# A two-lane recurrent transformer on one core: from a hand-staged schedule with DRAM round trips to an order list-placed at build time

## The chip, the cores and the metric

The kernel runs on one core of one Trainium2 chip. The metric is the device time of one execution in microseconds (us); lower is better. A core has TensorE (PE; its weight loads are shown as PEld), VectorE (DVE), ScalarE (ACT), GpSimd (POOL) and SyncE (SP, which here only issues DMAs). Each engine runs its own instructions in order and waits for the others by semaphores.

## The reference, cut to what matters

Four layers, A B A B, each added to its input. All weights are bf16; both A layers use the same weights, and so do both B layers.

```python
def _A_ref(x, mem0, Wq, Wk, Wv, Wo, seg_len):      # 2048 rows in 64 segments of 32, 32 heads of 192, model width 640
    mem = mem0                                      # 8 memory rows
    for s in range(n_seg):
        h = concatenate([mem, xs])                  # 8 + 32 = 40 rows
        q, k, v = h @ Wq, h @ Wk, h @ Wv            # 640 -> 6144 each
        p = softmax(where(mask, q @ k.T * scale, -1e9))
        o = (p @ v) @ Wo                            # 6144 -> 640
        mem = o[:M]                                 # the next segment needs it
        outs.append(o[M:])

def _B_ref(x, w1, w2, w3, w4):                      # 640 -> 640 -> 640, 640 -> 1536 -> 640
    h = gelu(layernorm(x) @ w1)
    hs = (four column groups of h, shifted by +1, -1, +2, -2 rows) @ w2
    x1 = x + hs
    return x1 + gelu(layernorm(x1) @ w3) @ w4

x = x + A(layernorm(x)); x = x + B(layernorm(x)); x = x + A(layernorm(x)); x = x + B(layernorm(x))
```

The memory makes layer A a recurrence over 64 segments: no segment can start before the one ahead of it has its first eight output rows.

## The kernel before

**Two lanes.** A step t runs segment t of the first A layer (lane 0) together with segment t - 6 of the second A layer (lane 1, `D_LAG` = 6). Both use the same weights, so the 2 x 40 rows form one moving operand of 80 columns. There are 64 + 6 = 70 steps. In the first six and the last six steps only one lane has a segment; the width stays 80.

**A step** goes over 8 groups of 4 heads. For a group, `st_proj` makes q and k transposed (30 matmuls of 80 columns each, L530) and v (10 matmuls of 384 columns, L568); `st_scores` adds the mask by a matmul of the identity with a constant (L600) and the scores (L610); `st_softmax` takes the row maximum (DVE, L617), its negative (L619), four exponentials with their sums (ACT, L624), reciprocal and product (DVE, L630 and L632); `st_pt` transposes P (L642) and copies it to SBUF (ACT); `st_pv` makes the heads' output (L654, L659), which DVE copies to `oT`; `st_wo` adds 30 matmuls of 80 columns to `psy` (L675), a PSUM tile that lives for the whole step and is cleared by a matmul with zeros (L515). The stages of neighbouring groups are interleaved by hand. `a_finish` copies the memory columns of `psy` into the next step's `hT` (ACT, L494); the next step's first q and k wait for that.

**Layer B** runs every second step on a chunk of 64 rows of each lane (128 rows), cut into stages that stand as fillers behind the groups (`b2x_stages`). The rows go through DRAM: `a_xnew` transposes the step's output back, adds the residual and stores it to `x1d` or `x3d` (SP queue); a later chunk loads it again as `xw` (ACT queue, `sA`), takes two layer norms in a row, and stores its result to `x2d`, which lane 1 loads again as `xs1`.

**Weights.** Wq, Wk, Wv and Wo are cut into 64 half-group units of 480 KB; 37 stay in SBUF after their first load (`get_w`, L357), 27 are streamed in every step. Ahead of the first step the 27 are copied inside DRAM to `wS`, where a partition's 3840 bytes lie together (`nc.scalar.dma_start`, ACT queue); the streams read `wS` (L362). The weights of B are copied to `wB` likewise and streamed per chunk in 13 pieces (L334). All streams use one ring of six 480 KB buffers, `wst`, and the SP queue.

**Order.** The instructions stand in each engine's queue in about the order in which Python issued them; `tc.high_priority()` lifts `a_finish`. What the fillers load and compute is thereby fixed against the groups. An SP instruction whose buffer isn't free holds what stands behind it, and a DVE instruction whose DMA hasn't landed holds every later DVE instruction.

Of the kernel before, what the change touches and what calls it, by code (L numbers as in the profile page):

```python
# [14 lines left out]
B2X = 1  # L15
D_LAG = 6 if B2X else 4
HG = 4
# [5 lines left out]
RING_BUFS = 6  # L23
N_RES_HALVES = 37 if B2X else 26
B_SLOT_SHIFT = 0
B_LOAD_Q = "act"
RELAYOUT = 1
LAZY_RES = 1
PT_EARLY = 0
LN_SPLIT = 1  # L30
B_SHARED_RING = 1
RINGB_BUFS = 2
RES_GROUP0_FIRST = 0
SM_ACCUM = 1
PIPE_DEEP = 1
V_TRANSPOSE = 0
PREP_DMA_Q = "sp"
LN_NORM_POOL = 0
DEFER_XNEW = 1
OT_EVAC_ENG = "dve"  # L40
KT_EVAC_ENG = "dve"
B_WSTAT = 0
HS_SEQ = 1
XROW_DELAY = 0
KZ_ENG = "dve"
XS_MERGE = 0
DBG_T_LIMIT = 0
DBG_DO_A = 1
DBG_DO_B = 1
DBG_PRINT_POOLS = 0  # L50
# [3 lines left out]
def kernel(  # L54
# [26 lines left out]
    assert Dm % P == 0 and F % P == 0 and Dh == 192 and H % HG == 0 and HG == 4  # L81
    assert SEG == 32 and M == 8 and S % SEG == 0
    assert Dm % 4 == 0 and (Dm // 4) % 32 == 0
# [3 lines left out]
    XS = 2 * SEG  # L87
    NS = XS + 2 * M
    MS = [XS, XS + M]
    XP = XS + 8  # L90
    scale = float(Dh) ** -0.5
    T_A = NSEG + D_LAG
    T = NSEG + D_LAG + (3 if B2X else 2)
    if B2X:
        assert D_LAG % 2 == 0 and NSEG % 2 == 0
    NP2 = NSEG // 2
    XB = 2 * XS
    WB2 = XS + 4
    WSZ = KC * GW
    assert WSZ == GC * Dm  # L100
    QD = Dm // 4
    WB = SEG + 4
    WBP = WB + 4

    def head_pieces(i):
        f0, f1 = Dh * i, Dh * (i + 1)
        res = []
        f = f0
        while f < f1:
            c = f // P  # L110
            p0 = f % P
            p1 = min(P, p0 + (f1 - f))
            res.append((c, p0, p1))
            f += p1 - p0
        return res

    PIECES = [(i, c, p0, p1) for i in range(HG) for (c, p0, p1) in head_pieces(i)]
    STRAD = sorted(set(c for (i, c, p0, p1) in PIECES if p1 - p0 < P))
    assert STRAD == [1, 4]
    SIDX = {c: n for n, c in enumerate(STRAD)}  # L120

    def w2_pieces():
        offs = [1, 3, 0, 4]
        res = []
        for gi in range(4):
            f, f1 = QD * gi, QD * (gi + 1)
            while f < f1:
                kc = f // P
                p0 = f % P
# [98 lines left out]
    def _cons_order():  # L228
# [11 lines left out]
        for g in range(NG):  # L240
            if g + 1 < NG:
                A(g + 1)
# [949 lines left out]
```

## Time and profile before

| | |
|---|---|
| median of 3 runs | 4447.67 us (4444.01 to 4458.48) |
| profiled execution, span of its instructions | 4440.8 us |
| PE busy | 3858.8 us (87%), 72349 matmuls |
| DVE / ACT / POOL busy | 2650.4 / 1988.4 / 578.7 us |
| DMA | 1232.59 MB, mean 278 GB/s |
| mean granted TensorE clock | 0.951 |

The profiled execution's own time isn't listed beside its span; the three runs lie 3.2 to 17.7 us above the span, the median 6.9 us. Times in a row of the timeline are microseconds from the first instruction: start, duration, engine, line, operation, what it writes and reads, shapes, count, and in brackets how long the engine had been idle and what ended that. A row may merge several instructions. A matmul's end is modelled; what counts for a stream of them is the distance from one start to the next.

### The profile page before, as it was taken

The page shows a single profiled execution, that of the slowest core. Times are in us where ns is not written, and L with a number is a line of the kernel's source. Part 1 is how long each engine was busy: PE and PEld are TensorE (multiplying, and loading weights), DVE is VectorE, ACT ScalarE, POOL GpSimd, SP SyncE. Part 2 cuts the span into 40 slices and gives each one's busy share as a digit, 9 for nine tenths or more (in the row PEclk, how much of TensorE's full clock was granted, in tenths as well). Part 3 has the DMA queues.
Part 4 walks back from the last instruction along what each step waited for, and adds up shares of the span by engine and source line. Part 5 has one row for each costly group of instructions (what it writes and reads, how often), then busy time and mean ns, then how long its engine had stood idle before and what let it go on. Part 6 is the DMA issues. An engine that isn't in the chain of part 4 may idle for free. (4 is left out here: it accounts for less than half of the span.)

```text
span 4440.8 us, 168838 instructions
## 1 busy us (share of the span) xinstructions
PE 3858.8 (87%) x72349; PEld 3433.7 (77%) x72420; DVE 2650.4 (60%) x7089; ACT 1988.4 (45%) x7427; POOL 578.7 (13%) x1578
## 2 busy tenths in 40 slices
PE   2898989899889898888888889888889988999995
PEld 2787878788778787777787778787788877888883
DVE  1455656666666666665666666666566666566554
ACT  1444444444444444444444444444444444444442
POOL 2111111111111111111111111111111111111110
PEclk7999999999999999999999999999999999999997
DMA  9887878888788888887878888788788888888784
GB/s 357 296 275 250 275 270 278 283 287 283 270 284 284 287 283 276 276 286 268 282 271 282 284 286 280 273 273 273 268 280 278 282 284 292 282 280 276 267 279 161
DMA packets 404193, 1232.59 MB, mean 278 GB/s; under 512 B 47080, under 2 KB 88176, under 8 KB 403440
## 3 DMA queue, kind: packets, MB, share of 16 engines
q1 hardware_dynamic: 378632, 1190.97, 78.6%
q10 hardware_dynamic: 21016, 23.76, 1.7%
q8 instruction: 566, 9.27, 0.8%
q0 software_dynamic: 3792, 7.05, 0.5%
q14 instruction: 187, 1.53, 0.1%
HBM read 1202.10 MB, written 38.50 MB: 279 GB/s over the span
## 5 line engine op out<-in xcount | busy, mean ns | idle before, releaser
L624 ACT ACTIVATE Pm<-pss,nb 80x80 bf16<-80x80 f32 x2240 | 699.6, 320 | 297.7 <-DVE nb L619 210.6
L568 PEld LDWEIGHTS <-hT 128*80 128x80 bf16 x5600 | 616.6, 118 | 209.5 <-issue 2.4
L372 ACT CAST V<-psv 80x384 bf16<-80x384 f32 x1120 | 507.2, 479 | 358.3 <-PE psv L568 278.4
L568 PE MATMUL psv<-wv,hT 128*80 128x384 bf16 x3500 | 663.5, 327 | 0.8 <-DMA wv<-in_A_Wv_dram 0.7
L374 DVE CAST oT<-pso 128x480 bf16<-128x480 f32 x560 | 367.7, 657 | 476.1 <-PE pso L659 474.0
L530 PEld LDWEIGHTS <-wst 128*128 128x128 bf16 x14700 | 637.3, 104 | 4.1 <-DMA wst<-wS 3.1
L374 DVE CAST kT<-psk 128x480 bf16<-128x480 f32 x560 | 364.8, 651 | 421.0 <-PE psk L530 419.3
L592 POOL COPY Vz<-V 80x128 bf16<-80x128 bf16 x560 | 169.7, 303 | 2878.0 <-ACT V L372 2865.6
L530 PE MATMUL psq<-hT,wq 128*128 128x80 bf16 x10500 | 496.9, 207 | 30.1 <-ACT hT L494 17.9
L530 PEld LDWEIGHTS <-wq 128*128 128x128 bf16 x10500 | 455.0, 103 | 38.7 <-issue 29.3
L372 ACT CAST qT<-psq 128x480 bf16<-128x480 f32 x560 | 307.5, 549 | 386.3 <-PE psq L530 384.6
L675 PE MATMUL psy<-oT,wst 128*128 128x80 bf16 x7350 | 360.2, 204 | 122.6 <-DVE oT L374 121.0
L675 PE MATMUL psy<-oT,wo 128*128 128x80 bf16 x9450 | 444.8, 204 | 2.1 <-DMA wo<-in_A_Wo_dram 2.1
L624 ACT ACTIVATION_READ_ACCUMULATOR Pm<-pss,nb 80x1 f32 x2240 | 442.5, 198 | 0.0
L675 PEld LDWEIGHTS <-wst 128*128 128x128 bf16 x7350 | 317.6, 101 | 151.2 <-issue 146.9
L568 PE MATMUL psv<-wst,hT 128*80 128x384 bf16 x2100 | 417.0, 330 | 0.8 <-DMA wst<-wS 0.8
L530 PE MATMUL psk<-hT,wst 128*128 128x80 bf16 x8400 | 411.9, 206 | 1.8 <-DMA wst<-wS 1.8
L530 PE MATMUL psk<-hT,wk 128*128 128x80 bf16 x8400 | 408.1, 205 | 3.0 <-DMA wk<-in_A_Wk_dram 3.0
L675 PEld LDWEIGHTS <-wo 128*128 128x128 bf16 x9450 | 387.5, 102 | 2.7 <-DMA wo<-in_A_Wo_dram 2.6
L372 ACT COPY PT<-pst 80x320 bf16<-80x320 bf16 x560 | 242.4, 433 | 273.2 <-PE pst L642 224.7
L610 PEld LDWEIGHTS <-qT 128*80 128x80 bf16 x3360 | 228.1, 123 | 170.5 <-issue 116.6
L374 DVE CAST kTz<-psk 64x160 bf16<-64x160 f32 x1120 | 351.9, 314 | 10.3
(122 smaller groups left out, 5892.4 us busy)
## 6 DMA issues: line engine op xcount, KB each, us to landing
wst<-wS SPq DMA_DIRECT2D x1890, 480.0 KB, 4.9
wst<-wB SPq DMA_DIRECT2D x395, 480.0 KB, 5.2
wst<-wB SPq DMA_DIRECT2D x71, 320.0 KB, 4.5
x1d<-xs SPq DMA_DIRECT2D x64, 80.0 KB, 4.0
xs<-x2d SPq DMA_DIRECT2D x64, 80.0 KB, 3.6
x3d<-xs SPq DMA_DIRECT2D x64, 80.0 KB, 3.7
xw<-x1d ACTq DMA_DIRECT2D x31, 160.0 KB, 3.6
x2d<-xw SPq DMA_DIRECT2D x31, 160.0 KB, 5.5
```

The lines of the kernel that those rows point to most:

```text
L372: nc.scalar.copy(out=out_ap, in_=in_ap)
L374: nc.vector.tensor_copy(out=out_ap, in_=in_ap)
L530: nc.tensor.matmul(out=psq[:, c, :], lhsT=w[:, kc, cc * P:(cc + 1) * P], rhs=hT[:, kc, :], start=(kc == 0), stop=(kc == KC - 1))
L568: nc.tensor.matmul(out=psv[:], lhsT=hT[:, kc, :], rhs=wv[:, kc, :], start=(kc == 0), stop=(kc == KC - 1))
L592: nc.gpsimd.tensor_copy(out=vz[:, :, 0, 0:64], in_=V3[:, SS, 0:64])
L610: nc.tensor.matmul(out=o_, lhsT=l_, rhs=r_, start=False, stop=(n == len(ops) - 1))
L624: nc.scalar.activation(out=E[:, i, :], in_=pss[:, i, :], func=ACT.Exp, bias=nb[:], scale=scale, accum_out=sums[:, i:i + 1])
L675: nc.tensor.matmul(out=cx.psy[:, m, :], lhsT=wo[:, cc, m * P:(m + 1) * P], rhs=oT[:, c, :], start=False, stop=last)
```

## The change

The kernel is rewritten around a build-time planner; what is computed stays the same.

- **Recording and placement.** `Plan.add` records each operation with its engine, an assumed duration, a due time and the buffers that it reads and writes. `Plan.place` then fixes the order on all engines: it goes forward in assumed time, and of the operations of an engine that could start soonest it takes the one with the earliest due time. A load is assumed to take 1.6 us, its size at 350 GB/s and 0.4 us. Only the order is kept; on the chip the engines still wait by semaphores.
- **Lanes.** The lag is 5, so there are 69 steps. Memory and segment of a lane lie together (40 columns), and a step with one lane uses 40 columns only (steps 0 to 4 and 64 to 68).
- **Mixer rows on chip.** The step's output columns go from `psy` to `yTB` (DVE). A chunk transposes `yTB` and adds the residual `xres`, which POOL loaded. The two layer norms in a row become one pass with two scale columns. `x1d` and `x3d` are gone. Lane 1's new columns are written to `hT` straight from the chunk's result (`chunk_end`); `x2d` remains, in bf16, as the residual. Lane 0's next two segments are normalised and transposed with the chunk.
- **Weights.** No copy in DRAM: both resident and streamed units are read from the input tensors, whose contiguous runs are 768 bytes (q, k, v, w1, w3) or 1280 bytes (Wo, w2, w4). Only w1 is copied once, to `w1d` (POOL), with its columns in another order. The ring is split: five buffers for A (`RING_A`), one for B (`RING_B`). B has 12 units per chunk, w2 now in five column groups rather than eight pieces; the second w2 unit takes five DMAs.
- **Smaller things.** The mask is added by DVE in one operation with scaling and minimum (`tensor_tensor_reduce`), in place of the mask matmul, the maximum and its negative. The zero matmul for `psy` is gone: the first Wo matmul starts the tile. K and V are written once in a layout that holds zeros where the heads of 192 straddle 128 partitions; POOL's two copies per group (`Vz`) are gone. PSUM is split by class (`PSUM_POOLS`).

```diff
-D_LAG = 6 if B2X else 4
...
-RING_BUFS = 6
-N_RES_HALVES = 37 if B2X else 26
...
-RELAYOUT = 1
...
-    x1d = dram.tile([S, Dm], f32, name="x1d")
...
-            nc.scalar.dma_start(out=w_view(wS[stream_idx[u_]], kind), in_=w_src(kind, g, hf))
...
-        nc.tensor.matmul(out=cx.psy[:], lhsT=zer[:, :], rhs=zer[:, 0:1].to_broadcast([P, KC * NS]),
-                         start=True, stop=False)
...
-        nc.tensor.matmul(out=pss[:], lhsT=ident[0:NS, 0:NS], rhs=maskb[:], start=True, stop=False)
...
-                stores.append(lambda: nc.sync.dma_start(out=x1d[SEG * segs[0]:SEG * (segs[0] + 1), :], in_=xo[0:SEG, :]))
...
-                {"sp": nc.sync, "act": nc.scalar, "pool": nc.gpsimd}[B_LOAD_Q].dma_start(
-                    out=xw[2 * j0 + Lb:2 * j1:2, :], in_=src[t0_ + j0:t0_ + j1, :])
-                if kp < NP2:
-                    nc.gpsimd.dma_start(out=xl_c[Lb:4:2, :], in_=src[TOK * kp + TOK - 2:TOK * kp + TOK, :])
...
+LAG = 5
+HG = 4
+N_RES = 37
+RING_A = 5
+RING_B = 1
+STEP = 48.0
+PSUM_POOLS = {"y": 1, "P": 3, "S": 2, "B": 2}
+OT_BUFS = 4
+V_BUFS = 3
+LAT = 0.2
+PE_LAT = 0.25
+DMA_RATE = 350.0e3
...
+                lim = m + (0.12 if e == "PE" else 0.05)
+                s, o = min((so for so in vals if so[0] <= lim), key=lambda so: (so[1].due, so[1].i))
...
+            if o.dma:
+                srv = max(s + 1.6, srv) + o.dma / DMA_RATE
+                done = srv + 0.4
...
+                if o.dma:
+                    at = done
+                elif x.e == e:
+                    at = o.end
+                else:
+                    at = o.end + (PE_LAT if e == "PE" else LAT)
...
+            return resident[u]
+        b = Slotted("ra", None)
+        b.make = lambda: wring.tile([P, HSZ], bf16, name="wst", tag=f"ra{b.slot}")
+
+        def fn(op):
+            nc.sync.dma_start(out=w_view(T(b), kind), in_=w_src(kind, g, hf))
+        add("SP", 0.06, due, fn, w=(b,), dma=P * HSZ * 2, queue="wa")
...
+    def load_b(nm, a, e, due):
...
+        b = Slotted("rb", None)
+        b.make = lambda: wring.tile([P, HSZ], bf16, name="wstB", tag=f"rb{b.slot}")
...
+        ln = lanes(t)
+        both = len(ln) == 2
+        c0 = 0 if 0 in ln else L1
+        N = NS if both else L1
...
+                        w, o = wv(), T(pq)
+                        for cc in range(GCH):
+                            for kc in range(KC):
+                                nc.tensor.matmul(out=o[:, hf * GCH + cc, 0:N], lhsT=w[:, kc, cc * P:(cc + 1) * P],
+                                                 rhs=h[:, kc, c0:c0 + N], start=(kc == 0), stop=(kc == KC - 1))
+                    add("PE", mm_us(N, k=GCH * KC), due, fn, r=(wb, *hk), a=(pq,))
+                if kind == "q":
...
+                nc.vector.tensor_tensor_reduce(out=o, in0=o, in1=maskt[:].unsqueeze(1).to_broadcast([N, HG, N]),
+                                               scale=-scale, scalar=3.0e38, op0=ALU.add, op1=ALU.min,
+                                               accum_out=sm_[0:N, 0:1])
+            add("DVE", dve_us(HG * N) + 0.1, hi - 4, f1, r=(pss,), w=(pss, smk))
...
+            for hf in range(2):
+                due = base + STEP - 1 + 0.02 * g if g >= NG - OT_BUFS + 1 else s0 + 2.0 * sl
+                wb, wv = load_unit(t, ("o", g, hf), s0 + (1.9 if g < NG - 1 else 1.2) * sl + 0.1 * hf)
...
+            def fm(op):
+                nc.scalar.copy(out=hn[:, :, m0:m1], in_=T(psy)[:, :, m0:m1])
+            add("ACT", act_us(KC * (m1 - m0)), due, fm, r=(psy,), w=(mk,))
...
+            for l in ln:
+                xc = 0 if l == 0 else L1 + M
+                nc.vector.tensor_copy(out=yv[:, :, l, t0:t0 + SEG], in_=T(psy)[:, :, xc:xc + SEG])
+        add("DVE", len(ln) * dve_us(KC * SEG), due + 4, fy, r=(psy,), w=(B("yTB", t % 2),))
...
+        def ft(op):
+            o = T(ps1)
+            for m in range(KC):
+                nc.tensor.transpose(out=o[:, m, :], in_=yTB[:, m, 0:XB], identity=ident[:, :])
+        add("PE", mm_us(128, k=KC), D(0.05), ft, r=(B("yTB", 0), B("yTB", 1), B("yTB", "h"), B("fin")), w=(ps1,))
...
+        def fx(op):
+            nc.vector.tensor_tensor(out=xw[:], in0=T(ps1)[:].rearrange("p k f -> p (k f)"), in1=xres[:], op=ALU.add)
+        add("DVE", 0.81, D(0.05), fx, r=(ps1, B("xres")), w=(xk,))
...
+                def fx0(op, s=s, j=j):
+                    nc.scalar.copy(out=hT[s % 4][:, :, 0:SEG], in_=T(psl2)[:, :, 32 + SEG * j:32 + SEG * (j + 1)])
+                add("ACT", act_us(KC * SEG), D(0.12), fx0, r=(psl2,), w=(B("hT", s % 4, "x0"),))
...
+            add("POOL", 0.9, D(1.55), fst, r=(B("xo"),), w=(B("x2d", c),) if lane == 0 else (), dma=(b - a) * Dm * 2)
...
+                def fc(op, a=a, b=b, o0=o0, tt=tt):
+                    pv = T(ps4)[:].rearrange("p k (w l) -> p k l w", l=2)
+                    d0 = L1 + M + o0
+                    nc.scalar.copy(out=hT[tt % 4][:, :, d0:d0 + b - a], in_=pv[:, :, 0, a:b])
+                add("ACT", act_us(KC * (b - a)), D(1.55) + (0.0 if o0 else 1.0), fc, r=(ps4,), w=(B("hT", tt % 4, key),))
...
+    placed = plan.place()
+    ctx.enter_context(tc.manual_schedule())
+    for o in placed:
+        o.fn(o)
```

Three places where the order matters. First DVE at the head of an even step, before: `xs` and `xw` are rows that come from DRAM, `ln_st` to `lnrs` their statistics, `kT` the group's keys.

```order
L401 BN_STATS ln_st<-xs_50056 32x6 x2
L401 BN_STATS ln_st<-xw 128x6
L402 BN_AGGR lnmv_p_50069<-ln_st 32x2
L401 BN_STATS ln_st<-xw 128x6
L403 TENSOR_SCALAR lnrs_p_50070<-lnmv_p_50069 32x1
L401 BN_STATS ln_st<-xl_c 4x6
L402 BN_AGGR lnmv_b_50193<-ln_st 128x2
L401 BN_STATS ln_st<-xl_c 4x6
L403 TENSOR_SCALAR lnrs_b_50194<-lnmv_b_50193 128x1
L374 CAST kT<-psk 128x480
```

And DVE at the same place in the changed kernel (`psx` is the transposed output, `xres` the residual, `lnx` the four look-ahead rows and lane 0's next rows):

```order
L652 CAST yTB<-psy 128x5x32 x2
L518 CAST kT_115<-psk 128x2x2x80
L524 CAST kT_115<-psk 64x2x80 x2
L794 TENSOR_TENSOR xw<-psx,xres 128x640
L798 TENSOR_TENSOR lnx<-psl,lnx 4x640
L569 ISA pss,sm_128<-pss,mask_78 80x320
L569 ISA sm_128 80x1
L663 BN_STATS st_146<-xw 128x6 x2
L664 BN_AGGR st_146<-st_146 128x2
...
L824 BN_STATS st_147<-lnx 96x6 x2
...
L582 RECIPROCAL sm_128<-sm_128 80x4
L583 TENSOR_TENSOR Pm_120<-Pm_120,sm_128 80x320
```

Before, the keys' copy (last row) stands behind the statistics of three loads. Now the first group's keys stand ahead of the chunk's rows, which come from PSUM; the statistics follow that group's mask, and what is still loaded (`xres`, `lnx`) is asked for a step ahead.

Second the SP queue at the start of a step with a chunk, before (`wS`, `wB`: the copied weights):

```order
L334 DMA wst<-wB 128x1920
L702 DMA x1d<-xs_66233 32x640
L705 DMA x3d<-xs_66233 32x640
L460 DMA xs_69176<-in_A_x_dram 32x640
L362 DMA wst<-wS 128x1920
L469 DMA xs_69175<-x2d 32x640
L362 DMA wst<-wS 128x1920 x2
L334 DMA wst<-wB 128x1920
```

and in the changed kernel (`wst`: the ring of five, `wstB`: the single buffer):

```order
L427 DMA wst<-in_A_Wq_dram 128x5x384
L427 DMA wst<-in_A_Wv_dram 128x5x384
L449 DMA wstB<-w1d 128x5x256
L427 DMA wst<-in_A_Wo_dram 128x3x640
L457 DMA wstB<-in_B_w_dram 128x3x640
L427 DMA wst<-in_A_Wk_dram 128x5x384
L427 DMA wst<-in_A_Wq_dram 128x5x384
L427 DMA wst<-in_A_Wv_dram 128x5x384
L457 DMA wstB<-in_B_w_dram 128x640
L460 DMA wstB<-in_B_w_dram 32x640 x4
```

The row stores and loads have left SP; each `wstB` load now waits until the unit ahead of it has been used.

Third PE in the changed kernel between the two w1 units of a chunk (`psh`), each row the first of a run of like matmuls (15 `psh`, 15 for each of the two `psy` and for `psq`, 5 for each `psv`, 4 `pst`, 4 and 2 `pss`):

```order
L873 MATMUL psh<-vT,wstB 128x128
...
L623 MATMUL psy<-oT_124,wo_0_162 128x80
...
L623 MATMUL psy<-oT_124,wo_1_163 128x80
...
L503 MATMUL psq<-hT_111,wq_1_170 128x80
...
L535 MATMUL psv<-wst,hT_111 80x384
...
L535 MATMUL psv<-wv_1_171,hT_111 80x384
...
L591 MATMUL pst<-ident,Pm_121 80x80
...
L558 MATMUL pss<-kT_115,qT_113 80x80
...
L558 MATMUL pss<-kT_115,qT_113 80x160
...
L873 MATMUL psh<-vT,wstB 128x128
```

Before, the two units stood behind two neighbouring groups, and the second one's load had a buffer of the ring of six. Now 65 matmuls and transposes stand between the two, and the second one's load is issued when the first unit is done.

The same queue at the end of a step, again the first row of each run (15, 15, 4, 8, 15, 15, 15):

```order
L623 MATMUL psy<-oT_126,wo_0_190 128x80
...
L623 MATMUL psy<-oT_126,wst 128x80
...
L591 MATMUL pst<-ident,Pm_121 80x80
...
L605 MATMUL pso<-PT_123,V_117 128x80
...
L623 MATMUL psy<-oT_127,wst 128x80
...
L623 MATMUL psy<-oT_127,wo_1_195 128x80
...
L503 MATMUL psk<-hT_111,wk_0_159 128x80
```

Sixty Wo matmuls that could have run earlier (two groups, 30 each; the first 30 end just ahead of this piece) now stand ahead of the last group's `pst`; behind that `pst`, nothing stands between it, its `pso`, its Wo and the next step's first keys.

1730 lines of the change are left out of this document (748 added, 982 removed).

## The prediction

> **What bounds the kernel now.** I read the span and PE's share first, then the steps' starts, then one group in the middle, then the stalls.
>
> ```profile
> span 4440.8 us, 168838 instructions
> PE 3858.8 (87%) x72349; PEld 3433.7 (77%) x72420; DVE 2650.4 (60%) x7089; ACT 1988.4 (45%) x7427; POOL 578.7 (13%) x1578
> 30.10 0.53 PE L515 MATMUL psy<-zer 128*128 128x400 bf16 x1
> 143.72 0.34 PE L515 MATMUL psy<-zer 128*128 128x400 bf16 x1
> 4295.86 0.34 PE L515 MATMUL psy<-zer 128*128 128x400 bf16 x1
> ```
>
> L515 starts each step's output tile: the first, second and last of 70. So the span is 30.1 us of start, 113.6 us for step 0, 68 steps in 4152.1 us (61.06 us each), and 144.9 us for the last step with the last chunks.
>
> PE's own work in a step follows from the distances between starts. This is one whole group with a unit of w3 (`psh`) behind it:
>
> ```profile
> 2005.28 0.70 PE L530 MATMUL psq<-hT,wst 128*128 128x80 bf16 x15
> 2005.82 0.70 PE L530 MATMUL psq<-hT,wq 128*128 128x80 bf16 x15
> ...
> 2007.43 0.98 PE L568 MATMUL psv<-wv,hT 128*80 128x384 bf16 x5
> 2008.25 0.98 PE L568 MATMUL psv<-wst,hT 128*80 128x384 bf16 x5
> 2009.06 0.32 PE L642 MATMUL pst<-ident,Pm 80*80 80x80 bf16 x4
> 2009.21 0.71 PE L675 MATMUL psy<-oT,wst 128*128 128x80 bf16 x15
> ...
> 2010.29 0.31 PE L654 MATMUL pso<-PT,V 80*128 80x80 bf16 x4
> ...
> 2010.57 1.00 PE L1056 MATMUL psh<-v2T,wst 128*128 128x128 bf16 x15
> 2011.42 0.30 PE L600 MATMUL pss<-maskb,ident 80*80 80x320 bf16 x1
> 2011.56 0.31 PE L610 MATMUL pss<-kT,qT 128*80 128x80 bf16 x4
> ...
> 2011.85 1.24 PE L530 MATMUL psq<-hT,wq 128*128 128x80 bf16 x30
> ```
>
> Fifteen matmuls of 80 columns take 0.54 us (36 ns each), five of 384 columns 0.815, fifteen of 128 columns 0.85 (56 ns), the 320-column mask 0.14. From 2005.28 to 2011.85 less 0.85 is 5.72 us per group, 45.8 for eight; the rest of a step is 0.6 for transposes and the zero matmul and half a chunk, 5.5 (85 matmuls of 128 columns at 56 ns, 20 pairs of 512 and 128 columns at some 0.28 in proportion, 15 transposes). That is 51.9 of 61.06 us: 9 us per step are waits and slow clock. Two kinds stand out. At the head of an even step:
>
> ```profile
> 2051.14 0.50 DVE L401 BATCH_NORM_STATS2 ln_st<-xw 128x6 f32<-128x320 f32 x1 [2.29 <-DMA xw<-x3d]
> ...
> 2053.52 0.64 DVE L374 CAST kT<-psk 128x480 bf16<-128x480 f32 x1
> ...
> 2054.21 0.43 PE L610 MATMUL pss<-kT,qT 128*80 128x80 bf16 x4 [5.63 <-DVE kT L374]
> 2054.44 1.00 PE L530 MATMUL psq<-hT,wst 128*128 128x80 bf16 x12
> ```
>
> DVE stands at statistics of rows that are still on their way from DRAM, the keys wait behind them, and PE idles 5.63 us; the next twelve matmuls then take some 66 ns each, not 36. And at every step's end PE waits along the recurrence:
>
> ```profile
> 2030.05 0.32 PE L642 MATMUL pst<-ident,Pm 80*80 80x80 bf16 x4
> ...
> 2030.45 0.42 ACT L372 COPY PT<-pst 80x320 bf16<-80x320 bf16 x1 [1.28 <-PE psy L675]
> 2030.92 0.30 PE L654 MATMUL pso<-PT,V 80*128 80x80 bf16 x4
> ...
> 2031.41 0.66 DVE L374 CAST oT<-pso 128x480 bf16<-128x480 f32 x1 [1.51 <-PE pso L659]
> 2032.12 0.70 PE L675 MATMUL psy<-oT,wst 128*128 128x80 bf16 x15 [0.58 <-DVE oT L374]
> ...
> 2033.39 0.23 ACT L494 CAST hT<-psy 128x80 bf16<-128x80 f32 x1 [2.52 <-PE psy L675]
> ...
> 2033.67 0.70 PE L530 MATMUL psq<-hT,wq 128*128 128x80 bf16 x15 [0.31 <-ACT hT L494]
> ```
>
> So PE bounds the work, and dependences, not bandwidth, set the rest: DMA moves 1232.59 MB, 278 GB/s.
>
> **The change, part by part.** *PE work of a full step.* The mask matmul goes (0.14 per group), the scores and outputs stay: 5.57 us per group, 44.5 for eight. The zero matmul and the step's own transposes go. A chunk has 85 matmuls of 128 columns and 30 transposes (6.4 us with one set of 96 columns), w2 and w4 as 34 matmuls of 320 columns (4.6 us): 11 us, 5.5 per step. Sum 50.0 us, 1.9 less than before.
>
> *The step's end.* From the rows above: PT is ready 0.72 us after `pst` has issued (0.25 + 0.42 + 0.05), nothing covers it; `oT` 0.91 us after `pso` (0.2 + 0.66 + 0.05), nothing covers it; the memory columns 0.48 us after Wo (0.2 + 0.23 + 0.05), covered in every second step by a w3 unit. The last `pss` to `pst` takes 3.0 us if the new DVE operation takes about 0.55, and two V halves and 60 Wo matmuls, 2.96 us, cover that. I charge 1.9 us. The operation's nearest rows bound it:
>
> ```profile
> L617 DVE TENSOR_REDUCE mx<-pss 80x1 f32<-80x320 f32 x560 | 268.0, 479 | 58.2 <-PE pss L610 53.0
> L421 DVE TENSOR_TENSOR g_sq<-g_sq,psh 128x384 f32<-128x384 f32 x179 | 96.9, 541 | 0.9
> ```
>
> A one-input pass of 320 columns takes 479 ns, a two-input one of 384 columns 541; with a sum to read out up to 0.8 us. At 0.8 a step costs 0.25 us more. Elsewhere DVE hides it: it is busy 60% of the time, and the groups' DVE work hardly changes.
>
> *The head of an even step.* The 5.63 us stall and the slow clock behind it go: the chunk's rows come from PSUM, the keys stand ahead of them. If `xres`, loaded a step earlier, were late all the same, the stall would return, at some 3 us per step. POOL's Vz copies and SP's row traffic were beside the path: nothing.
>
> *B's single buffer.* This is the new wait. A unit's load is issued when the unit ahead has been used. The PE work between neighbouring units of a chunk, counted with the distances above, is 3.7, 4.8, 3.2, 9.0, 6.9, 5.6, 1.5 (plus 1.6 of the step's end), 6.2, 5.7, 4.5, 4.3 and, to the next chunk, 35 us. How long a load takes:
>
> ```profile
> wst<-wS SPq DMA_DIRECT2D x1890, 480.0 KB, 4.9
> wst<-wB SPq DMA_DIRECT2D x395, 480.0 KB, 5.2
> xs<-x2d SPq DMA_DIRECT2D x64, 80.0 KB, 3.6
> wq<-in_A_Wq_dram SPq DMA_DIRECT2D x10, 480.0 KB, 9.6
> ```
>
> With 0.25 us for release and semaphore, 3.6 us is the least (an 80 KB transfer), 5.2 the median of `wB` with other loads ahead of it. 9.6 is the row with the new form, 768-byte runs, but from the start, where all queues are full. I take 4.5 with the release, nearer the least: a lone buffer's load often finds fewer ahead of it. The shortfalls are 0.8, 1.3, 1.4 and 0.2, and 1.4 more for the second w2 unit's further four issues: 5.1 per chunk, 2.6 per step. At 3.85 it is 1.5, at 5.45 it is 5.2. Behind a late unit all of PE waits, since its order is fixed. A's ring has at least 6 us from a buffer's release to its next use, so it covers itself below that.
>
> By the Trainium skill's page "DMA: Bandwidth & Descriptors", section "Anatomy of one DMA — SWDGE (gpsimd) path", a transfer takes about 2.0 us and its bytes at 436 GB/s, here 3.1 us as an estimate, given there for POOL's queue; B's shortfall would be about 1 us per step and the time some 95 us below mine. The 4.9 and 5.2 us above speak against it.
>
> *DMA.* A streams 27 x 0.49 = 13.3 MB per step, B 2.8, rows 0.1: 16.2 MB. What the chip gives short runs is seen at the start, where the resident units and the copies to `wS` have them:
>
> ```profile
> 60.00:70.00 10.00, 0.00 (x0) 0.00 (x0) 0.00 (x0) 0.00 (x0) 0.00 (x0) 0.50 1.09 377
> 110.00:120.00 10.00, 8.27 (x176) 7.33 (x173) 4.54 (x12) 4.20 (x18) 1.12 (x4) 1.00 1.08 363
> 800.00:1600.00 800.00, 718.95 (x13645) 641.19 (x13655) 501.29 (x1342) 373.87 (x1402) 103.93 (x285) 0.97 0.83 282
> ```
>
> At 360 GB/s (last column) 16.2 MB take 45 us, less than the 50 of PE, so full steps aren't bound by it. One-lane steps are: at 40 columns PE needs 29 us (each matmul half of 36 ns) to 44.5 (no gain) beside half a chunk, DMA 45; I take 46. Without a gain they would cost 50 to 55 like the others, some 70 us in all. Step 1 has no chunk: 13.3 MB are 37 us, PE 29 to 44.5 and the step's end 1.9; I take 41.
>
> *The start.* ACT's first work waited 88 us for the copies to `wS`:
>
> ```profile
> 87.99 1.28 ACT L372 ACT_TABLE_LOAD x1 [87.99 <-DMA wS<-in_A_Wo_dram]
> ```
>
> That goes. Step 0 now loads all 64 units, 31.5 MB, 87 us at 360 GB/s; with 3 us ahead it ends at 90, not 143.7.
>
> *The tail.* The last chunk runs alone with one buffer: 12 loads at 5 us and a share of 0.8 us of PE each, 70 us, with some 5 us of norms ahead, and five units of the chunk before, 25 us: 100 us behind the last step (84 before).
>
> Sum: 90 + step 1 at 41 + 3 x 46 + 59 full steps at 55.0 (50.0 + 1.9 + 2.6 + 0.5 for small waits) = 3245 + 5 x 46 = 230 + 100 = 3844 us of span. The median stands 6.9 us above the profiled span: **3850 us**.
>
> **The rivals.** *(1) B's loads hide.* If loads land in 3.6 us or find slack, a step is 52.4 to 53: 3690 to 3730. For it: the planner's own spacing; against it: 4.9 and 5.2. *(2) DMA binds.* If the SP queue with short runs gives only the 282 GB/s of the steady row, a step is 57.5: 90 + 68 x 57.5 + 100 = 4100. For it: 282 at a share of 0.83 leaves 340 at a full one; against it: 363 from 110 us on, when ACT's queue was done. The same page, section "Why small descriptors are slow (HBM only)", gives each packet some three cycles of overhead; for 768 against 3840 bytes that is some 8% as an estimate, 48 us a step, and the rows at the start don't show it. *(3) Slower than before.* If a lone load takes what the row with the new form shows, a chunk takes 12 x (9.6 + 0.25 + 0.78) = 128 us, 64 per step, and the tail 150: 90 + 41 + 67 x 64 + 150 = 4570. It decides from about 9.3 us per load on. For it: the 9.6; against it: that row stands under the full queues of the start.
>
> **How the numbers follow.** Forecast, PE with B's shortfall: 0.60. Rival 1: 0.19; rival 2: 0.15; rival 3: 0.04; no gain because some other wait of 6 us per step returns: 0.02. The forecast's bounds, 3.85 to 5.45 us per load, give 3780 to 4000; rival 1 sets the low end, 3690, and part of rival 2 the high end, 4110. Faster by over 0.3% (what a measurement can tell): 0.95; the same: 0.01; slower: 0.04.
>
> **What would show it.** Steps of 55 us, 50 of it PE's work; PE's waits led by `wstB`, 2 to 3 us per step, then by PT and `oT`; no wait on keys over 3 us and a clock near 1; 315 GB/s in the middle; step 0 over by 90 us; some 100 us behind the last step. I am wrong if PE waits for `wst`, if landings exceed 6 us, or if a full step is under 53 or over 58 us.

## The result and the profile after

The changed kernel takes **4179.1 us** (median of 4 runs, 4166.0 to 4201.7); the kernel before took 4445.9 in the same session. The ratio is **0.940 (0.936 to 0.943)**: 6% faster, where the prediction had 13%. The time lies 329 us above the forecast and 69 above the upper end of its range. The profiled execution is the slowest of the four, 4201.7 us; all sums below are made against its span, 4200.0 us. Times are medians of the fast runs: one of the four runs of the ninth kernel below took 8468 us and is left out.

The head of the page after:

```profile
span 4200.0 us, 162257 instructions
...
PE 3679.9 (88%) x70351; PEld 3232.6 (77%) x70351; DVE 2221.0 (53%) x6403; ACT 1960.1 (47%) x7380; POOL 280.8 (7%) x489
...
PEclk7999999999999999999999999999999999999995
```

The steps are counted by ACT's copy of the memory columns, which ends each of them. From the timeline (start, duration, engine and line; in brackets the idle time before and who ended it), the ends of steps 0, 1, 4, 63 and 67:

```profile
95.59 0.19 ACT L640 CAST hT<-psy 128x40 bf16<-128x40 f32 x1 [3.85 <-PE psy L623]
...
140.64 0.19 ACT L640 CAST hT<-psy 128x40 bf16<-128x40 f32 x1 [1.85 <-PE psy L623]
...
302.17 0.19 ACT L640 CAST hT<-psy 128x40 bf16<-128x40 f32 x1 [0.76 <-PE psy L623]
...
3835.23 0.19 ACT L640 CAST hT<-psy 128x40 bf16<-128x40 f32 x1 [2.59 <-PE psy L623]
...
4040.80 0.19 ACT L640 CAST hT<-psy 128x40 bf16<-128x40 f32 x1 [2.08 <-PE psy L623]
```

| part | predicted us | measured us | over |
|---|---|---|---|
| step 0 | 90 | 95.6 | 6 |
| steps 1 to 4 | 41 + 3 x 46 = 179 | 206.6 | 28 |
| 59 full steps | 55.0 each, 3245 | 59.88 each, 3533 | 288 |
| steps 64 to 67 | 184 | 205.6 | 22 |
| last step and tail | 146 | 159.2 | 13 |

So four fifths of the miss lie in the full steps, 4.9 us in each. What PE waits for (total us, times, longest):

```profile
PE y L948 <- DMA wstB<-in_B_w_dram: 120.5, 70, 3.7
PE psh L928 <- DMA wstB<-in_B_w_dram: 90.9, 46, 3.8
PE hs L896 <- DMA wstB<-in_B_w_dram: 72.0, 71, 3.8
PE psh L873 <- DMA wstB<-w1d: 53.9, 35, 3.3
PE psy L623 <- DVE oT L611: 53.5, 70, 0.9
PE pso L605 <- ACT PT L596: 44.7, 70, 0.8
PE pst L591 <- DVE Pm L583: 14.6, 30, 1.0
PE psk L503 <- ACT hT L640: 13.0, 39, 0.7
```

The four `wstB` rows sum to 337 us, 9.6 per chunk; counted in the 59 full steps alone they are 4.4 us per step. The step's end (the other four rows) is 126 us, 1.9 per full step. PE waits 4.4 us in the whole run for any one form of A's `wst` at most, and not at all for keys: those parts of the prediction held. The windows view of the middle has the rest (stretch and its length, busy time of PE, PEld, DVE, ACT and POOL, then granted clock, DMA share, GB/s):

```profile
1600.00:3000.00 1400.00, 1254.86 (x23876) 1127.49 (x23874) 771.47 (x2158) 675.66 (x2505) 88.60 (x150) 0.95 0.88 275
```

The clock is 0.95, and the prediction had "a clock near 1". In a full step 5.6 us are at half speed; 0.7 of them fall into PE's idle times, the other 4.9 cost 2.5 us of work. What is left of the 59.9 us without waits and slow clock is 51.1 us.

How one wait and the slow clock hang together is seen at the end of a step, in the timeline of PE:

```profile
2088.51 0.70 PE L623 MATMUL psy<-oT,wst 128*128 128x80 bf16 x15 [0.87 <-DVE oT L611]
2089.04 0.70 PE L623 MATMUL psy<-oT,wo 128*128 128x80 bf16 x15
2092.28 1.78 PE L928 MATMUL psh<-vT,wstB 128*128 128x128 bf16 x15 [2.53 <-DMA wstB<-in_B_w_dram]
2093.85 1.21 PE L503 MATMUL psk<-hT,wk 128*128 128x80 bf16 x15
2094.85 1.20 PE L503 MATMUL psk<-hT,wst 128*128 128x80 bf16 x15
```

and in that of SP's queue:

```profile
2081.74 0.37 SPq L427 DMA_DIRECT2D wst<-in_A_Wq_dram  x1
2083.83 0.37 SPq L427 DMA_DIRECT2D wst<-in_A_Wv_dram  x1
2085.44 0.37 SPq L427 DMA_DIRECT2D wst<-in_A_Wk_dram  x1
2086.28 0.37 SPq L451 DMA_DIRECT2D wstB<-in_B_w_dram  x1
```

The lone buffer comes free and is filled again from 2086.28 on, with three loads of A issued in the 4.5 us before it. The unit starts at 2092.28, 6.0 us later; PE has little else to do in between and idles 2.53 us. Then fifteen matmuls take 1.78 us where they took 1.00 in the profile before, and groups of 80 columns 1.2 instead of 0.70: half speed. The clock's record has half speed from 2090.70 to 2097.53 us: it began 1 us into the wait and outlasted it by 5.

In the middle of the trace (400 to 3700 us) a full-sized load of B landed, counted from the end of its issue, by the loads of A in flight at that moment:

| loads of A in flight | 0 | 1 | 2 | 3 | 4 |
|---|---|---|---|---|---|
| loads of B | 35 | 39 | 91 | 99 | 14 |
| median landing, us | 3.1 | 3.5 | 4.0 | 5.5 | 5.75 |

How many a unit finds is largely set by the planned order: the last unit of w3 found three in all 28 chunks of this stretch, the first of w4 none in all 28.

In the rows of DMA issues (count, size, median us to landing) all 480 KB loads of B have 4.8, since units that were issued early and that nobody waits for are among them:

```profile
wst<-in_A_Wq_dram SPq DMA_DIRECT2D x483, 480.0 KB, 5.5
wstB<-in_B_w_dram SPq DMA_DIRECT2D x315, 480.0 KB, 4.8
...
wstB<-w1d SPq DMA_DIRECT2D x35, 320.0 KB, 5.2
```

From issue to landing, the issue's own time included, the units before which PE waits are those that land late: the second of w1 5.2 us, the second of w2 5.4 (its five issues alone take 2.2), the last of w3 5.7, the second and the last of w4 6.0 and 6.4. SP doesn't hold them back: for each of the twelve units the issue starts 0.25 to 0.34 us (median) behind the start of the last matmul that used the buffer.

### The profile page after: what moved, and what is told of

It is laid out like the page before. It is cut to its first block, busy times and chain, and to the rows that moved or that the text cites. A ratio compares the mean times of both kernels' runs of the same rounds, so it can differ in the third digit from the quotient of the medians.

```text
span 4200.0 us, 162257 instructions
## 1 busy us (share of the span) xinstructions
PE 3679.9 (88%) x70351; PEld 3232.6 (77%) x70351; DVE 2221.0 (53%) x6403; ACT 1960.1 (47%) x7380; POOL 280.8 (7%) x489
## 4 chain that ended last, share of the span: by engine, by line
PE 67%; DMA 25%; issue 2%; SPq 2%; ACT 2%; DVE 1%; POOL 0%; ACTq 0%; POOLq 0%; DVEq 0%
DMA wstB<-in_B_w_dram 19%; PE psv L535 16%; PE psk L503 13%; PE psq L503 12%; PE psy L623 8%; DMA wstB<-w1d 4%; PE psh L928 3%; PE y L948 3%; PE pso L605 3%; PE pss L558 3%; PE pst L591 2%; PE psh L873 1%; PE hs L896 1%; SPq L460 1%; ACT Pm L577 1%
## 5 line engine op out<-in xcount | busy, mean ns | idle before, releaser
L577 ACT ACTIVATE Pm<-pss,sm 80x80 bf16<-80x80 f32 (+1 forms) x2208 | 673.3, 314 | 186.8 <-DVE sm L569 186.2
L540 ACT CAST V<-psv 80x384 bf16<-80x384 f32 (+1 forms) x1104 | 522.1, 474 | 507.4 <-PE psv L535 504.2
L535 PEld LDWEIGHTS <-hT 128*80 128x80 bf16 (+1 forms) x5520 | 586.4, 117 | 213.7 <-issue 15.8
L535 PE MATMUL psv<-wv,hT 128*80 128x384 bf16 (+1 forms) x3105 | 611.5, 332 | 2.3 <-DMA wv<-in_A_Wv_dram 2.1
L535 PE MATMUL psv<-wst,hT 128*80 128x384 bf16 (+1 forms) x2415 | 483.6, 332 | 0.7 <-DMA wst<-in_A_Wv_dram 0.4
L503 PE MATMUL psk<-hT,wk 128*128 128x80 bf16 (+1 forms) x9315 | 441.8, 205 | 17.6 <-ACT hT L640 13.0
L623 PE MATMUL psy<-oT,wo 128*128 128x80 bf16 (+1 forms) x10350 | 454.1, 200 | 2.2 <-DVE oT L611 1.5
L503 PE MATMUL psq<-hT,wq 128*128 128x80 bf16 (+1 forms) x9315 | 440.5, 203 | 5.8 <-DMA wq<-in_A_Wq_dram 5.7
L577 ACT ACTIVATION_READ_ACCUMULATOR Pm<-pss,sm 80x1 f32 (+1 forms) x2208 | 437.0, 198 | 0.0
L503 PEld LDWEIGHTS <-wk 128*128 128x128 bf16 x9315 | 396.8, 104 | 40.4 <-issue 22.2
```

What stands on the lines that cost most here:

```text
L503: nc.tensor.matmul(out=o[:, hf * GCH + cc, 0:N], lhsT=w[:, kc, cc * P:(cc + 1) * P], rhs=h[:, kc, c0:c0 + N], start=(kc == 0), stop=(kc == ...
L535: nc.tensor.matmul(out=o[0:N, :], lhsT=h[:, kc, c0:c0 + N], rhs=w[:, kc, :], start=(kc == 0), stop=(kc == KC - 1))
L540: nc.scalar.copy(out=v_runs(V_, hf)[0:N], in_=T(pv)[0:N, :].rearrange("n (a b) -> n a b", a=2))
L577: nc.scalar.activation(out=Pb[0:N, i, 0:N], in_=o[0:N, i * N:(i + 1) * N], func=ACT.Exp, bias=sm_[0:N, 0:1], scale=-1.0, accum_out=sm_[0:N ...
L623: nc.tensor.matmul(out=o[:, m, c0:c0 + N], lhsT=w[:, cc, m * P:(m + 1) * P], rhs=o_[:, hf * GCH + cc, 0:N], start=st, stop=True, skip_grou ...
```

## The experiments

**Theory 1**: B's one buffer makes the miss, through the waits for `wstB` and the slow clock behind them. **Theory 2**: the loads in short runs are held to some 275 GB/s, and the waits only show it. Each kernel below is the changed one with the edit shown; its ratio is to the kernel before, timed beside it. The changed kernel stands at 0.940.

### 1. The planner's constant for a load

```
-                srv = max(s + 1.6, srv) + o.dma / DMA_RATE
+                srv = max(s + 3.0, srv) + o.dma / DMA_RATE
```

> One number of the planner is changed: a load's assumed fixed part, 3.0 us in place of 1.6 (assumed landing 4.8 us in place of 3.4 for 480 KB). Buffers, bytes and work stay the same; only the order moves, and the PE work between two neighbouring units of B becomes at least 4.1 us (5.0 mostly) in place of at least 1.5 (3.2 to 4.8 at four places). Theory 1 (PE waits because B's single buffer can't be refilled within the work that stands between two units, and the waits halve the clock): PE's waits for wstB fall from 11 us per chunk to under 3, the mean clock rises above 0.96, a full step falls from 59.9 to 54-55 us, the time to 3840-3920 us. Theory 2 (the loads' rate binds: 16.2 MB per step at the 275 GB/s that the profile shows are 58.9 us): the order changes nothing, 4150-4200 us, the waits move to other tiles.

Measured: 3934.8 us, **0.883 (0.877 to 0.888)**, 15 us above what Theory 1 gave and far below Theory 2's. Nothing but the order differs. PE's waits:

```profile
PE psh L928 <- DMA wstB<-in_B_w_dram: 65.9, 59, 3.8
...
PE y L948 <- DMA wstB<-in_B_w_dram: 45.2, 37, 3.7
PE hs L896 <- DMA wstB<-in_B_w_dram: 38.6, 62, 3.7
...
PE psh L873 <- DMA wstB<-w1d: 13.4, 17, 3.3
```

and the middle window:

```profile
1600.00:3000.00 1400.00, 1310.14 (x25583) 1173.67 (x25583) 827.55 (x2314) 731.09 (x2686) 97.06 (x158) 0.99 0.93 295
```

The four sum to 163 us where they were 337 (4.7 per chunk, not under 3 as expected), the clock is 0.99, and the same short runs now move 295 GB/s. A full step is 55.6 us. The loads did not land earlier (their median is 5.6 us): the units were put further apart.

### 2. and 3. Two buffers for B

```
-RING_A = 5
-RING_B = 1
+RING_A = 4
+RING_B = 2
```

> Two buffers for B and four for A, the same memory and bytes. Theory 1: waits for wstB nearly vanish (a load is issued one unit earlier); A's ring of four has some 4.5 to 5 us at its tightest places against landings of 5.3 us, so small waits for wst appear, about 1 us per step. A full step 54-56 us, time 3850-3950 us. Theory 2: 4150-4200 us, waits moved from wstB to wst.

Measured: 4052.9 us, **0.909 (0.905 to 0.912)**, a full step of 57.8 us: between the two expectations. B's waits are down to 11 us, and A's came in their place, 219 us in these three rows, where some 1 us per step was expected:

```profile
PE psk L503 <- DMA wst<-in_A_Wk_dram: 97.8, 89, 2.5
PE psq L503 <- DMA wst<-in_A_Wq_dram: 92.9, 110, 3.0
...
PE psv L535 <- DMA wst<-in_A_Wv_dram: 27.9, 37, 2.0
```

The buffer can be taken from the resident halves instead, at 3% more bytes to stream:

```
-N_RES = 37
-RING_B = 1
+N_RES = 36
+RING_B = 2
```

> Two buffers for B, five for A, paid for with one resident unit: 28 units of A are streamed per step in place of 27, 16.7 MB in place of 16.2 (+3%). Theory 1: waits for wstB nearly vanish, a full step 53.5-55 us, 3800-3900 us, at some 310 GB/s. Theory 2: the bytes set the time, so it gets slower by up to 3%: 4200-4300 us, never above 280 GB/s.

Measured: 3823.1 us, **0.857 (0.853 to 0.862)**, a full step of 54.3 us. What PE waits for most, with no `wstB` in the lead:

```profile
PE psy L623 <- DVE oT L611: 49.9, 68, 0.8
PE psq L503 <- DMA wst<-in_A_Wq_dram: 46.2, 53, 2.1
PE pso L605 <- ACT PT L596: 23.5, 44, 0.6
```

The middle window of this run:

```profile
1600.00:3000.00 1400.00, 1336.53 (x26230) 1201.20 (x26227) 849.33 (x2383) 743.96 (x2754) 108.24 (x169) 0.99 0.97 311
```

More bytes in less time, 311 GB/s, and time and step where Theory 1 had them: Theory 2 falls.

### 4. B's weights loaded once

The first unit's load stays, and all later units of B compute with that buffer.

```
+            if once:
+                return once["b"], view0
```

> B's weights are loaded once, for the first unit of the first chunk, and every later unit computes with what stands in that buffer: the kernel leaves out all of B's other weight loads (2.8 MB per step) and its mixer results are not the reference's. It shows what PE's steps cost without any of B's loads. Theory 1: a full step 53-54 us (50.0 of PE's work, 2 at the step's end, 1 to 2 small), a clock of 0.97 or more in the middle, 3650-3720 us in all. Theory 2: the remaining 13.4 MB per step at 275 GB/s are 48.7 us, under PE's 50, so it also gets to 3650-3750; this run tells the price of all of B's loads together, and not the theories apart.

Measured: 3708.3 us, **0.832 (0.828 to 0.835)**, a full step of 52.9 us. This is what the steps cost without B's loads (the planner, with fewer loads to place, wrote another order). Of 52.9 us the step's end takes 1.6, the slow clock 0.3, other waits 0.2: 50.8 us are left for PE's work, which the prediction had at 50.0.

### 5. Zero matmuls in the waits

How much of the harm is the clock? PE is given work for the time in which it waits for B.

```
+    def warm(o, start, k):
+        for _ in range(k):
+            nc.tensor.matmul(out=o, lhsT=zer[:], rhs=ident[:, 0:80], start=start, stop=True, skip_group_check=True)
...
+                warm(o[:, 0, 0:80], True, {9: 56}.get(a, 0))
```

> The changed kernel with 180 more matmuls per chunk, zeros times 80 columns into the unit's own PSUM tile (they add nothing to the result), ahead of just those units of B before which PE was seen to wait: 40 ahead of the second w1 unit, 14 ahead of the second w2 and w4 units, 56 ahead of the last w3 and w4 units. At 36 ns each that is 6.5 us per chunk, put into waits of 11 us. Theory 1a (of B's single buffer half of the harm is the slow clock that each idle of 2 to 4 us leaves behind): the half-speed stretches fall from 314 us (of the 3300 us from 400 on) to under 150, the full step from 59.9 to 57.0 to 58.5 us, the whole to 4000 to 4100 us, though PE has more to do and the loads land no earlier. Theory 1b (the waits alone are the harm, the clock costs little): the step stays at 59.9 to 61 us, the whole at 4180 to 4260 us.

Measured: 4116.6 us, **0.926 (0.923 to 0.929)**, a full step of 58.3 us, 1.6 less. The step is within what Theory 1a gave, the whole 17 us above it and well below Theory 1b's. Its middle window:

```profile
1600.00:3000.00 1400.00, 1326.19 (x26610) 1201.10 (x26607) 792.53 (x2220) 694.71 (x2569) 93.44 (x156) 0.98 0.90 282
```

The clock rose from 0.95 to 0.98 and the half-speed stretches fell from 314 to 102 us. In the full steps the waits for `wstB` went from 4.4 to 1.1 us per step, about as much as the 3.2 us of zero matmuls that fill them; what the slow clock costs PE's work went from 2.5 to 0.8 us, the 1.6 gained. With 6300 matmuls more, which serve nothing, the kernel is faster. So the clock is a harm of its own, 2.5 us per step in the changed kernel, beside the 4.4 of the waits themselves.

### 6. The relayout put back

ACT's queue copies the streamed units at the start, as before, and a load reads runs of 3840 bytes. The core of it:

```
+    for u in streamed:
+        nc.scalar.dma_start(out=w_view(wS[streamed.index(u)], u[0]), in_=w_src(*u))
...
-            nc.sync.dma_start(out=w_view(T(b), kind), in_=w_src(kind, g, hf))
+            nc.sync.dma_start(out=T(b)[:], in_=wS[streamed.index(u)])
```

> The changed kernel with the relayout put back: at the start ACT's queue copies the 27 streamed units of A and the units of w2, w3 and w4 to DRAM in the order in which SBUF wants them, and the streamed loads read runs of 3840 bytes, the second w2 unit with one load and not five. Everything else is as changed, RING_B = 1 too. If the short runs are what makes B's loads land late (theory 3): the landing of 480 KB falls from 4.8 to about 4 us, the full step from 59.9 to 57 us or less, the start grows by some 48 us, as before: 4179 - 59 x 2.9 + 48, about 4055 us. If what counts is how many loads stand ahead on the queue (theory 1): landings stay over 4.5 us, the full step is 58.9 to 59.9 us (the second w2 unit's further issues gone), and the start makes the whole slower: 4170 to 4230 us.

Measured: 4108.3 us, **0.924 (0.921 to 0.926)**: faster than the changed kernel, though not by Theory 3's mark. Step 0 ends at 147.0 us for 95.6, so the start costs 51; a full step is 57.6 us, 2.3 less. PE's waits for B in it:

```profile
PE y L962 <- DMA wstB<-wB: 81.4, 58, 3.5
PE psh L942 <- DMA wstB<-wB: 76.5, 43, 3.7
...
PE psh L887 <- DMA wstB<-w1d: 41.6, 34, 3.3
PE hs L910 <- DMA wstB<-wB: 32.3, 37, 2.9
```

B's waits are 232 us instead of 337, most of the difference at `hs` and `y`. The second w2 unit, one load now, lands after 3.8 us instead of 5.4; the last units of w3 and w4 after 5.5 and 5.8 instead of 5.7 and 6.4. So both accounts hold in part: the short runs make landings a little longer, and most of their length stays. That it comes from the loads in flight is what the table above shows; no run took A's loads away and left B's. With one buffer for B, leaving the relayout out cost more in the steps than it saved at the start. With two it wasn't tried.

### 7. One-lane steps 80 columns wide

```
-        N = NS if both else L1
+        N = NS
```

> The changed kernel with the one-lane steps (the first five and the last five) 80 columns wide again, the absent lane's columns zero or stale. The prediction said that 40 columns buy little, since those steps are bound by DMA (13.3 to 16.2 MB each): then steps 1 to 4 and 64 to 68 grow by 0 to 2 us each, the whole by at most 20 us. If PE's work bounds them, they grow from 52.5 us on average to the full step's 59.9, about 67 us in all: 4245 us.

This expectation misstates the prediction, which had put the 40 columns at some 70 us in all. Measured: 4242.3 us, **0.953 (0.950 to 0.956)**, 63 us more than the changed kernel; steps 1 and 2 take 51.2 and 57.2 us for 45.1 and 56.7, step 3 61.5 for 48.7; in the two profiles steps 1 to 4 and 64 to 67 take 57 us more together. PE's width does bound those steps, and the prediction's price was about right.

### 8. Two buffers and the planner's constant

```
-N_RES = 37
-RING_B = 1
+N_RES = 36
+RING_B = 2
...
-                srv = max(s + 1.6, srv) + o.dma / DMA_RATE
+                srv = max(s + 3.0, srv) + o.dma / DMA_RATE
```

> Two buffers for B (RING_B = 2, N_RES = 36) together with the planner's 3.0 us for a load instead of 1.6. Alone the first gave 3823 us with some 1.5 us of waits for A's loads left per step (46 us in all ahead of psq), the second 3935. If the constant works for A's loads as for B's (issue and use planned further apart): 3770 to 3800 us and the waits for wst gone. If the rate is now what holds A's loads back (312 GB/s at a busy share of 0.97 of the queues): 3810 to 3835 us, no difference.

Measured: 3786.3 us, **0.851 (0.849 to 0.854)**, the fastest version that computes everything. Full steps are 53.9 us, 0.4 less than in the third. Between the two profiled executions lie 48 us (37 between the medians): 25 in the full steps, 19 in the one-lane steps, 4 in the tail. PE's waits:

```profile
PE psy L623 <- DVE oT L611: 51.2, 71, 0.9
PE psq L503 <- DMA wst<-in_A_Wq_dram: 38.1, 47, 2.5
PE pso L605 <- ACT PT L596: 23.6, 44, 0.8
PE psk L503 <- ACT hT L640: 20.7, 67, 0.4
```

and the middle window:

```profile
1600.00:3000.00 1400.00, 1335.24 (x26303) 1202.64 (x26300) 853.52 (x2394) 745.46 (x2761) 108.03 (x169) 0.99 0.97 312
```

The time is where the first branch had it, but its reason is not: the waits for `wst` did not go (38.1 of 46.2 us).

### 9. and 12. All resident halves, paid for with an oT buffer

```
-RING_B = 1
+RING_B = 2
...
-OT_BUFS = 4
+OT_BUFS = 3
```

with the constant of 3.0 us:

> Two buffers for B with all 37 resident halves kept: the 3840 bytes per partition are made up by OT_BUFS = 3 instead of 4 (960 bytes) and what lay free; the planner's load constant is 3.0. So the streamed bytes are those of the change again, 3% fewer than with N_RES = 36. If the rate of 312 to 314 GB/s held A's loads back there (38.1 us of waits of psq and 10.0 of psk for wst): those waits fall by half or more and the step from 53.95 to 53.0 to 53.5 us, the whole from 3786 to 3730 to 3765. If the planner's spacing makes them, or if the third oT buffer was needed (a new wait of psy or of DVE for oT): 3775 to 3810 us.

Measured: 3923.4 us, **0.881 (0.879 to 0.884)**: 137 us slower than the eighth with fewer bytes, outside both branches. Two things differ from it, so the last run changes one: N_RES = 36 again, OT_BUFS = 3.

> The kernel with two buffers for B, N_RES = 36 and the planner's 3.0 us (3786 us), with OT_BUFS = 3 for 4 and nothing else. With N_RES = 37 besides, the whole had come to 3930 us, against the expectation: new were 31 us more of waits of pst for Pm and 23 more of pso for PT at the steps' ends, 37 of psv for wst, and half-speed stretches of 191 us for 68. If the third oT buffer makes them (the planner must place Wo earlier, and less is left to cover the softmax at a step's end): 3890 to 3940 us, the Pm waits over 40 us. If the other set of streamed units makes them (six halves of Wo among 27, not four among 28): 3775 to 3810 us, the Pm waits under 25 us.

Measured: 4080.4 us, **0.916 (0.913 to 0.919)**. The constant `OT_BUFS` makes the loss, and a larger one than expected (294 us against the eighth, where at most 154 were); the other resident half gave 157 us of it back in the ninth. The constant sets two things: the number of oT buffers, and by `if g >= NG - OT_BUFS + 1` for how many groups of a step the planner keeps Wo back to the step's end, two in place of three. No run parts them. PE's waits in the twelfth:

```profile
PE psq L503 <- DMA wst<-in_A_Wq_dram: 83.1, 77, 2.7
PE psy L623 <- DVE oT L611: 52.3, 69, 0.9
PE psh L928 <- DMA wstB<-in_B_w_dram: 50.2, 28, 3.1
PE pst L591 <- DVE Pm L583: 49.3, 35, 1.6
```

and its middle window:

```profile
1600.00:3000.00 1400.00, 1280.30 (x24277) 1144.86 (x24275) 787.94 (x2208) 692.05 (x2554) 99.82 (x156) 0.95 0.96 288
```

The wait for Pm is there as expected (49.3 us, 16.4 in the eighth), but it is the smaller part: waits for loads came back, and with them the slow clock. The planner wrote another order. Why that order meets its loads so much later was not followed further.

### 10. and 11. B's loads on another queue

```
-                nc.sync.dma_start(out=v, in_=w3_v[:, :, a * P:e * P])
+                nc.scalar.dma_start(out=v, in_=w3_v[:, :, a * P:e * P])
```

and the same for the other units; in the eleventh with POOL's queue, where the planner is told 1.0 us per issue (4.0 for the second w2 unit) instead of 0.06 (0.3).

> The changed kernel with B's loads issued by ACT's queue and not SP's; one buffer, the planner's 1.6 us and all else as changed. In the trace of the changed kernel a load of B lands 3.1 us after its issue with no load of A in flight, 3.8 with two, 5.1 with three, 5.5 with four. If it is the place behind them on the queue (theory 1c): on a queue of its own the landing falls to 3.3 to 4.2 us, the waits for wstB from 11 to under 6 us per chunk, the step from 59.9 to 57.5 us or less, the whole under 4030 us, as far as ACT, which stands at each issue until the buffer is free, delays nobody. If the DMA engines share out their rate among all that is in flight, whatever the queue (theory 1d): the landing stays at 4.6 to 5.2 us, the whole at 4150 to 4250 us.

> The same on POOL's queue, whose engine nobody waits for in the middle of a step. Theory 1c: landings of 3.3 to 4.2 us from the end of the issue, the whole under 4050 us unless POOL's own work of issuing such a load costs over 1 us, which no run has shown. Theory 1d: 4.6 to 5.2 us from the end of the issue, the whole at 4180 us or above.

The medians for two to four loads in flight in the first of these texts differ from the table above, which has the full-sized loads alone and counts every load of A. Measured: 4187.5 us, **0.939 (0.936 to 0.942)** on ACT's queue and 4347.8, **0.976 (0.972 to 0.980)** on POOL's. PE's waits in the ACT run:

```profile
PE pso L605 <- ACT PT L596: 113.7, 103, 3.0
PE y L948 <- DMA wstB<-in_B_w_dram: 111.5, 79, 3.9
PE psh L928 <- DMA wstB<-in_B_w_dram: 81.2, 55, 3.9
```

With no load of A in flight a full-sized load of B lands after 3.3 us there, with one after 3.3, with two after 4.1, with three after 5.9, with four after 5.6: near the figures of the shared queue (3.1, 3.5, 4.0, 5.5, 5.75). Theory 1d holds: what counts is how much is in flight, not which queue it stands on. The waits for B did fall, to 239 us, but ACT stands at each issue until the buffer is free, and PE waits 69 us more for PT. On POOL the landings are 3.2, 3.95, 4.0, 5.1 and 5.3 us; each issue of 480 KB takes POOL 0.8 to 0.9 us, and the waits for B rise to 424 us (`hs`, with the unit of five issues, has 190 of them).

## Why the prediction was right or wrong

**What bounds the kernel: right.** PE's work and dependences bound it before and after; the rate does not (311 GB/s in the third run, 275 in the changed kernel). PE's work was put at 50.0 us per step, the fourth run leaves 50.8 and the changed kernel 51.1. The step's end was 1.9 and measured 1.9. The new DVE operation was taken at 0.55 us with bounds of 0.48 and 0.8; it is 0.49 with a read-out of 0.14 behind it, and PE's wait for `Pm`, which comes from it, is 14.6 us in all. At the prediction's own distances the cover for it, two V halves and 60 Wo matmuls, is 3.8 us, not 2.96; nothing hangs on that.

**The head of an even step: right.** No wait for keys is left among PE's.

**The start: right.** It was to end at 90 us and ended at 95.6; the copies' cost was put at 53.7 us (143.7 less 90), and the sixth run shows 51.

**The one-lane steps: the gain right, the level and the bound wrong.** Some 70 us were claimed for the 40 columns, 63 measured. But steps 2 to 4 take 53.8 us, not 46: each has half a chunk with 3.4 us of B's waits in it, and the prediction charged those to full steps alone. With two buffers and the constant they take (195.8 - 45.1) / 3 = 50.2. Nor do the loads bind them: in the fourth run, with none of B's, they still take 49.5 us at 275 GB/s, while the eighth moves 339 GB/s there. PE is busy for 48 of the 49.5; a matmul of 40 columns starts 25 ns behind the one before it, not half of 36.

**B's single buffer: the mechanism right, the size wrong.** It is the step "I take 4.5 with the release, nearer the least: a lone buffer's load often finds fewer ahead of it". Only 35 loads of 278 found none. At the units with little work ahead, the ones that count, landings are 5.2 to 6.4 us (two of them over the 6 us that the prediction had named as a sign of being wrong). With the measured landings and 0.25 us of release, the prediction's own distances give shortfalls of 1.8, 2.5, 2.8, 0.6 and 2.3 us (the second units of w1 and w2, the last of w3, the second and last of w4): 10.0 per chunk, 5.0 per step for its 2.6; 4.4 were measured in the full steps. Its upper bound (5.45 us a load, 5.2 a step) held that. No row spoke for the choice below the middle, since `wst` and `wB`, the nearest in size and company, stood at 4.9 and 5.2.

The page "DMA: Bandwidth & Descriptors" of the Trainium skill, section "Anatomy of one DMA — SWDGE (gpsimd) path", had given 3.1 us as an estimate; the trace shows 3.1 for a load with nothing of A in flight and 5.75 with four. It is the price of a load alone. The Trainium skill's same page, section "Queues, rings and completion order", says that a load's semaphore write lands only after every earlier write of that DMA engine, across its queues; the tenth run, where another queue changed landings by 0.4 us at most, agrees, though engines that merely share out their rate would look the same.

**The slow clock behind the waits: not in the sum.** The prediction read the stall and the slow matmuls behind it in the profile before ("the next twelve matmuls then take some 66 ns each, not 36"), removed both, and gave the new waits no such tail. It cost 2.5 us per full step, nearly the whole shortfall that was charged. The fifth run gained 1.6 of them with matmuls that compute nothing.

So a full step is 51.1 of work, 4.4 of waits for B, 1.9 at its end and 2.5 of slow clock: 59.9 us. The predicted 55.0 had 50.0, 2.6, 1.9, nothing for the clock and 0.5 for small waits. The 4.9 us that it missed are the clock (2.5), B's waits (1.8) and PE's work (1.1), less the small waits.

**The tail: nearly right**, 159 us for the last step and the tail together, against 146; in the eighth run it is 113, so the lone buffer and the constant are 46 of them.

**The rivals.** The first (B's loads hide) is what the fourth run is and the eighth nearly, 3708 and 3786 us: its time was right for another kernel. The second predicted 4100, near the time that came: by luck, since its reason was wrong. Its one sign, a rate of 282 in the row before, was an outcome of PE's pace, as 275 is in the changed kernel. The third needed 9.3 us per load; the longest median of any group of B's loads that repeats is 7.3 (the ninth run).

**The parts of the change, by their worth.** The gain of 6% comes with a loss inside: `RING_B = 1` and the planner's 1.6 us per load cost 393 us against the eighth run.

## What to carry to other kernels

Where a buffer is alone, price its load by the loads that will be in flight at that moment, not by the least transfer of the trace; the rows for loads in like company were there, and the planned order largely says how many there will be. Most waits of 2 us or more on TensorE (44 of 53 here) cost their own length and a stretch at half speed, so charge both, and look at the granted clock first when a step comes out longer than work and waits together. In a planned order, the planner's figure for a load is a tuning knob of the first rank: one constant moved this kernel by 6%.

## What the runs showed of the hardware

- In the changed kernel, between 400 and 3700 us, half speed came in 70 stretches, 48 of 3.41 us and 22 of twice that. One began in or within 2 us behind 44 of the 53 idle times of PE of 2.0 to 3.3 us (30 of the 44 while PE still idled), and 9 of the 54 of 1 to 2 us.
- In these runs the busy share of the DMA engines didn't tell what they could move. The twelfth run has a share of 0.96 at 288 GB/s, the eighth 0.97 at 312, with the same form of load.
- A load of 480 KB landed 3.1 us after its issue with none of A's in flight and 5.75 with four of them; on a queue of its own (ACT's) it was 3.3 and 5.6.
- A matmul of 40 columns started 25 ns behind the one before it, one of 80 columns 36 ns.
